# Splitting the 128-row products of one 256-token MLP block into two 64-row tiles of the array

## The chip, the cores and the metric

The kernel runs on one core of one Trainium2 chip. Its time is the device time of one execution in microseconds (us); the comparison is between medians of repeated executions. Five things of the core matter here: TensorE (PE in the rows; PEld is its weight load), VectorE (DVE), ScalarE (ACT), the DMA queues that SyncE (SP) issues to, and the eight banks of PSUM into which TensorE writes.

## The reference, cut to what matters

An attention with a position bias gives x of 2304 tokens by 512; a gated MLP follows:

```python
def _moe_ref(x, w_in, w_out):        # x 2304 x 512, w_in 512 x 2048, w_out 2048 x 512
    h = x @ w_in
    sp = np.where(h > 20.0, h, np.log1p(np.exp(np.minimum(h, 20.0))))
    g = h * np.tanh(sp)
    return (g @ w_out).astype(np.float32)
```

## The kernel before

The first 313 us make the bias, the attention and, beside them, the split weights. The rest is the MLP, which is where the change lies. Each fp32 operand is held as a high and a low part in the type fp32r, and a product is three products: high by high, high by low, low by high.

The tokens are cut into five blocks of 512, 512, 256, 512 and 512 (`blocks`, numbered 0 to 4). The 2048 hidden columns are cut into 16 slices of 128. A *unit* is one slice of a block of 512 tokens, or two slices of the block of 256, so that it always fills a PSUM bank of 128 x 512. There are 72 units; block 2 (256 tokens) has units 32 to 39. For unit k, written H(k), G(k) and P(k) in this document:

- H(k), `hidden`: TensorE computes h of the unit (L553; in block 2, 24 products of 256 columns, in the others 12 of 512), ScalarE takes exp (L558), VectorE clamps it and forms e*(e+2) (L559, L560).
- G(k), `gate`: ScalarE takes a logarithm and an exponential (L568, L569), VectorE multiplies h by e (L570) and that by r (L571), ScalarE writes the high part ghi (L575), VectorE the low part glo (L576).
- P(k), `project`: 12 products of 512 columns add the unit to y (L591). After a block's last unit y is copied out by both engines (L608 on ScalarE, L610 on VectorE) and stored (L611).

The order is written out by hand, and each engine executes its own instructions in that order. One turn of the loop is: in some turns a piece of the next block's x, then H(k), P(k-3), G(k-1). The pieces for the next block: in the turn whose first slice is 6 (unit 35 in block 2), `load_x` and `load_r` issue the loads of x (L307) and of the softmax reciprocals r (L321) through SP's queue, behind whatever that queue still has to issue. In the turns with slice 8 and up (units 36 to 39 in block 2) `split_x` works ahead of H(k): for two of the four rows of x in a turn, first VectorE multiplies x by r (L534) and ScalarE writes the high parts xhi (L535), in units 36 and 37; then VectorE writes the low parts xlo (L537), in units 38 and 39. H(40), the first unit of block 3, reads xhi and xlo.

PSUM: `h_ps` has four banks for h, and a new h takes the bank that was released earliest; `y_ps` has four banks, y0 to y3, of which block 2 uses two. h of unit k is read for the last time by L570 in G(k).

The 64-row slices TOP and LOW already serve the attention's scores, where the two heads of a pair lie in the upper and lower 64 rows:

```python
    TOP, LOW = slice(0, 64), slice(64, P)
    heads = (TOP, KO), (LOW, KO - 64 if c < 4 else KO)
    for j in range(2):
        for s, (rows, k0) in zip(live[n], heads):
            pe.matmul(s[:, j, :SH], q[rows], raw[rows, k0 + j * SH:k0 + (j + 1) * SH], start=True, stop=True)
```

Of the kernel before, what the change touches and what calls it, by code (L numbers as in the profile page):

```python
# [7 lines left out]
F32 = mybir.dt.float32  # L8
# [3 lines left out]
ALU = mybir.AluOpType  # L12
# [5 lines left out]
DM, DFF = 512, 2048  # L18
NT = B * S
P = 128  # L20
# [10 lines left out]
TB = 512  # L31
NFC = DFF // P
# [12 lines left out]
def kernel(ctx: ExitStack, tc, qk, v, wb, w2, w_in, w_out, psia, psi4, rinv, eye, out):  # L45
    nc = tc.nc
    pe, dve, act, pool, sp = nc.tensor, nc.vector, nc.scalar, nc.gpsimd, nc.sync
# [131 lines left out]
    TOP, LOW = slice(0, 64), slice(64, P)  # L179
# [247 lines left out]
    def reach(t):  # L427

        left, right = 16 * t + 15, S - 16 * t
        n = max(left + 1, right)  # L430
        return left, right, n + n % 2
# [6 lines left out]
    for idx, t in enumerate(ts):  # L438
        spent["a"] += 1.0 + (1.9 if idx in SOFT_AT else 0.0)
        spent["v"] += (1.7 if idx in SOFT_AT else 0.0)  # L440
        n = reach(t)[2]
        price = {"v": 0.10 + 0.00072 * n, "a": 0.30 + 0.0008 * n}
        for cg in (3, 2, 1, 0):
            e = min(price, key=lambda k: spent[k] + price[k])
# [32 lines left out]
    for idx in range(NB + 2):  # L477
        if idx < NB:
            t = ts[idx]
            make_h(idx + 2)  # L480
            n = reach(t)[2]
# [36 lines left out]
    mp = sbuf("mp", 2, side="right")  # L518
    h_ps = psum("h_ps", 4, side="right")
# [21 lines left out]
    h_t, gs, ys = {}, {}, {}  # L541
# [2 lines left out]

    def hidden(blk, fs):
        n = blocks[blk][1]
        h = h_ps.tile([P, TB], F32, name="h")
        for u, f in enumerate(fs):
            g4, r = divmod(f, 4)
            k = 0  # L550
            for w, x in ((w_hi, x_hi[blk]), (w_lo, x_hi[blk]), (w_hi, x_lo[blk])):
                for d in range(HP):
                    pe.matmul(h[:, u * n:(u + 1) * n], w["i", g4, d][:, r * P:(r + 1) * P], x[:, d, :n],  # L553
                              start=(k == 0), stop=(k == 11))
                    k += 1

        e = mp.tile([P, TB], F32, name="e", bufs=3)
        act.activation(e, h, AF.Exp)  # L558
        dve.tensor_scalar(e, e, E20, None, op0=ALU.min)  # L559
        dve.scalar_tensor_tensor(e, e, 2.0, e, op0=ALU.add, op1=ALU.mult)  # L560
        h_t[blk, fs] = (h, e)
# [17 lines left out]
    def project(blk, fs):  # L579
        t0, n = blocks[blk]  # L580
        ghi, glo = gs.pop((blk, fs))
        nt = n // P
        if fs[0] == 0:
            ys[blk] = [y_ps.tile([P, DM], F32, name=f"y{t}") for t in range(nt)]
        for t in range(nt):
            for u, f in enumerate(fs):
                g4, r = divmod(f, 4)
                whi, wlo = w_hi["o", g4, r], w_lo["o", g4, r]
                c0 = u * n + t * P
                for k, (g, w) in enumerate(((ghi, whi), (ghi, wlo), (glo, whi))):  # L590
                    pe.matmul(ys[blk][t], g[:, c0:c0 + P], w,  # L591
                              start=(f == 0 and k == 0), stop=(f == NFC - 1 and k == 2))
        if fs[-1] == NFC - 1:
            for t in range(nt):

                if t % 2 == 0:
                    yo = convp.tile([P, 512, 2], U32, name="w64").bitcast(F32).rearrange("p f t -> p (f t)")
                part = yo[:, t % 2 * DM:(t % 2 + 1) * DM]
                rows = out[t0 + t * P:t0 + (t + 1) * P, :]
                if blk == len(blocks) - 1 and t == nt - 1:  # L600

                    dve.tensor_copy(part[:, :DM // 2], ys[blk][t][:, :DM // 2])
                    act.copy(part[:, DM // 2:], ys[blk][t][:, DM // 2:])
                    sp.dma_start(out=rows[:, :DM // 2], in_=part[:, :DM // 2])
                    act.dma_start(out=rows[:, DM // 2:], in_=part[:, DM // 2:])
                    continue
                if t % 2:
                    act.copy(part, ys[blk][t])  # L608
                else:
                    dve.tensor_copy(part, ys[blk][t])  # L610
                sp.dma_start(out=rows, in_=part)  # L611
            del ys[blk]


    step(NS)
    split_x(0, XPARTS)
    hidden(*units[0])
    step(NS + 1)
    step(NS + 2)
# [4 lines left out]
    y_ps = psum("y_ps", 1)  # L624
    alloc_weights(order[EARLY:MIDDLE], wq)
    gate(*units[0], 3)
    hidden(*units[1])
    gate(*units[1], 3)
    hidden(*units[2])

    for k in range(2, len(units) + LAG2):
        if k < len(units):
            blk, fs = units[k]
            f = fs[0]
            if blk + 1 < len(blocks):
                if f == 6:
                    load_x(blk + 1, xp)
                    x_lo[blk + 1] = xp.tile([P, HP, TB], F32R, name="xlo")
                    load_r(blk + 1, x_lo[blk + 1].bitcast(F32), 0, HP)

                if f >= 8:
                    split_x(blk + 1, XPARTS[f - 8:f - 8 + len(fs)])
            if k > 2:
                hidden(blk, fs)
        if k >= LAG2:
            project(*units[k - LAG2])
        if 2 <= k - 1 < len(units):
            gate(*units[k - 1], 2)
# [55 lines left out]
```

## Time and profile before

| | |
|---|---|
| time, median of 3 runs | 725.22 us (723.25 to 726.1) |
| profiled execution, its own time | 724.99 us |
| its span, first to last instruction | 723.2 us |
| PE busy, share of the span | 693.0 us, 96% |
| DVE busy | 509.4 us, 70% |
| ACT busy | 484.3 us, 67% |
| granted TensorE clock, mean | 0.991 of 2.4 GHz |
| block 2 on TensorE, start of H(32) to start of H(40) | 490.50 to 535.47 us |

Busy time is the union of an engine's instructions. A matmul's recorded length contains the way through the array, so matmuls that follow each other overlap in the records; the pace of a stream is read from starts, not from lengths. In a timeline row the first two numbers are the start and the length of a merged group; what stands in brackets is how long the engine was idle before it and what ended that. SPq is SP's queue.

### The profile page before, as it was taken

How to read it: one execution, taken by the hardware profiler on the slowest of the kernel's cores; microseconds unless marked ns; L12 is line 12 of the kernel's file. 1: busy time of each engine (PE TensorE's matmuls, PEld its weight loads, DVE VectorE, ACT ScalarE, POOL GpSimd, SP SyncE). 2: the span in 40 equal slices, each digit the busy share in tenths (PEclk: the TensorE clock that was granted, in tenths of full speed). 3: DMA queues.
4: the chain of work that ended last, by engine and by line, in shares of the span. 5: the costliest groups of instructions: out<-in, count | busy, mean ns of one | idle time of the engine just before them, and what ended most of it. 6: DMA issues, size and time to landing. Idle time of an engine off the chain costs nothing.

```text
span 723.2 us, 12806 instructions
## 1 busy us (share of the span) xinstructions
PE 693.0 (96%) x4768; PEld 508.0 (70%) x4768; DVE 509.4 (70%) x1080; ACT 484.3 (67%) x1059; POOL 11.5 (2%) x14
## 2 busy tenths in 40 slices
PE   6777999999999999989999999999999999999997
PEld 2214666666666666647888888889988888888886
DVE  7983888878888887548879666665577567665554
ACT  6895999898999999876666445544445454454443
POOL 0000110000000000300000000000000000000000
PEclk9998999999999999999999999999999999999999
DMA  4995458556735855204000030000603200010001
GB/s 152 325 309 173 143 195 271 181 162 204 243 134 196 260 203 206 68 17 127 1 0 1 0 118 1 0 1 1 176 0 106 41 0 1 1 58 1 0 2 58
DMA packets 43918, 74.79 MB, mean 103 GB/s; under 512 B 13904, under 2 KB 22608, under 8 KB 43856
## 3 DMA queue, kind: packets, MB, share of 16 engines
q1 hardware_dynamic: 43280, 73.75, 31.6%
q8 instruction: 37, 0.61, 0.3%
q10 hardware_dynamic: 576, 0.22, 0.1%
q14 instruction: 25, 0.20, 0.1%
HBM read 53.55 MB, written 20.40 MB: 102 GB/s over the span
## 4 chain that ended last, share of the span: by engine, by line
PE 69%; ACT 17%; DVE 6%; issue 3%; DMA 3%; SPq 1%; DVEq 0%; ACTq 0%
PE h L553 25%; PE y L591 25%; ACT pt L223 7%; PE o L282 6%; PE s L192 5%; ACT main L263 5%; PE bps L485 3%; PE tp L256 3%; DVE pt L208 2%; DMA bias_d<-bt 2%; PE tp L259 1%; PE o L286 1%; ACT main L268 1%; ACT tail L265 1%; ACT bt L467 1%
## 5 line engine op out<-in xcount | busy, mean ns | idle before, releaser
L208 DVE CUSTOM_DVE_ANT_0 pt<-s,bias 128x576 f32<-128x576 f32 (+1 forms) x160 | 115.9, 754 | 52.0 <-PE s L192 49.2
L223 ACT ACTIVATE pt<-pt,m 128x576 f32<-128x576 f32 x144 | 111.2, 772 | 26.6 <-DVE m L208 21.7
L591 PE MATMUL y<-who,ghi 128*128 128x512 f32 x288 | 112.2, 389 | 0.0
L591 PE MATMUL y<-wlo,ghi 128*128 128x512 f32 x288 | 112.1, 389 | 0.0
L591 PE MATMUL y<-who,glo 128*128 128x512 f32 x288 | 112.0, 389 | 0.0
L192 PE MATMUL s<-rawqk 64*128 64x288 f32 x640 | 108.2, 430 | 2.0 <-DVE m L208 1.9
L575 ACT CAST ghi<-e 128x512 fp32r<-128x512 f32 x72 | 44.7, 621 | 91.7 <-DVE e L571 91.6
L192 PEld LDWEIGHTS s<-rawqk 64*128 64x128 f32 x640 | 63.4, 186 | 44.2 <-DVE m L208 17.3
L558 ACT ACTIVATE e<-h 128x512 f32<-128x512 f32 x72 | 42.8, 596 | 63.0 <-PE h L553 62.8
L553 PE MATMUL h<-xhi,whi 128*128 128x512 f32 (+1 forms) x320 | 79.9, 370 | 1.7 <-ACT xhi L535 1.6
L553 PE MATMUL h<-xlo,whi 128*128 128x512 f32 (+1 forms) x320 | 79.9, 371 | 0.9 <-DVE xlo L537 0.8
L576 DVE TENSOR_TENSOR glo<-e,ghi 128x512 fp32r<-128x512 f32 x72 | 49.8, 691 | 43.5 <-ACT ghi L575 43.5
L559 DVE TENSOR_SCALAR e<-e 128x512 f32<-128x512 f32 x72 | 30.6, 426 | 69.7 <-ACT e L558 69.7
L553 PE MATMUL h<-xhi,wli 128*128 128x512 f32 (+1 forms) x320 | 79.5, 371 | 0.0
L282 PE MATMUL o<-main,vt 128*64 128x320 f32 (+1 forms) x512 | 77.5, 426 | 1.4 <-ACT tail L265 0.7
L256 PEld LDWEIGHTS tp<-ident,pt 64*128 64x128 f32 x1184 | 56.1, 139 | 20.5 <-ACT main L263 10.3
L263 ACT COPY main<-tp 128x512 f32<-128x512 f32 x128 | 67.6, 578 | 0.8 <-PE tp L256 0.3
L553 PEld LDWEIGHTS h<-xhi,whi 128*128 128x128 f32 x320 | 57.3, 188 | 14.0 <-ACT xhi L535 3.1
L256 PE MATMUL tp<-ident,pt 64*128 64x64 f32 x1184 | 62.5, 227 | 4.7 <-ACT main L263 2.2
L553 PEld LDWEIGHTS h<-xlo,whi 128*128 128x128 f32 x320 | 57.4, 190 | 11.8 <-DVE xlo L537 1.6
L553 PEld LDWEIGHTS h<-xhi,wli 128*128 128x128 f32 x320 | 57.4, 190 | 10.1
L591 PEld LDWEIGHTS y<-who,glo 128*128 128x128 f32 x288 | 54.1, 188 | 11.4
(54 smaller groups left out, 883.5 us busy)
## 6 DMA issues: line engine op xcount, KB each, us to landing
rawqk<-in_qk_dram SPq DMA_DIRECT2D x16, 672.0 KB
bias_d<-bt SPq DMA_DIRECT2D x36, 295.5 KB
w<-in_w_in_dram SPq DMA_DIRECT2D x16, 512.0 KB
w<-in_w_out_dram SPq DMA_DIRECT2D x16, 512.0 KB
vt<-in_v_dram SPq DMA_DIRECT2D x16, 320.0 KB
bias<-bias_d SPq DMA_DIRECT2D x16, 288.0 KB
out_dram<-w SPq DMA_DIRECT2D x17, 256.0 KB
bias<-bias_d SPq DMA_DIRECT2D x16, 256.0 KB
```

The costliest lines, as they stand in the source:

```text
L192: pe.matmul(s[:, j, :SH], q[rows], raw[rows, k0 + j * SH:k0 + (j + 1) * SH], start=True, stop=True)
L208: dve.tensor_tensor_reduce(out=halves(pt[rows, sl]), in0=s[rows, :, :SH], in1=halves(bt[rows, sl]), scale=-0.125, scalar=BIG, op0=ALU.add, ...
L223: act.activation(ps, ps, AF.Exp, bias=m[:, u:u + 1], scale=-1.0, accum_out=sums[i][:, k:k + 1])
L256: pe.transpose(tp[:, k * 64:k * 64 + 64], pt[rows, c0:c0 + P], ident[rows, rows])
L263: act.copy(main[:, :, :, q0:q0 + 64], tp.rearrange("p (h k q) -> p h k q", h=2, k=4))
L282: pe.matmul(o[h * 64:h * 64 + 64, :w], vt[:, h, k, :], main[:, h, k, :], start=(k == 0), stop=False, **kw)
L553: pe.matmul(h[:, u * n:(u + 1) * n], w["i", g4, d][:, r * P:(r + 1) * P], x[:, d, :n], start=(k == 0), stop=(k == 11))
L558: act.activation(e, h, AF.Exp)
L559: dve.tensor_scalar(e, e, E20, None, op0=ALU.min)
L575: act.copy(ghi, e)
L576: dve.tensor_tensor(glo, e, ghi.bitcast(F32), op=ALU.subtract)
L591: pe.matmul(ys[blk][t], g[:, c0:c0 + P], w, start=(f == 0 and k == 0), stop=(f == NFC - 1 and k == 2))
```

## The change

In block 2 (n = 256) each product over 128 rows becomes two over 64 rows, upper and lower, issued one behind the other, with a bank each. The two halves of h are added (ScalarE copies the lower half to e, VectorE adds it to the upper half in PSUM) ahead of the exponential. The halves of y go to y0/y2 and y1/y3 and are added when block 2 is copied out. The other blocks keep their products.

```diff
     def hidden(blk, fs):
         n = blocks[blk][1]
-        h = h_ps.tile([P, TB], F32, name="h")
+        rows = (TOP, LOW) if n < TB else (slice(0, P),)
+        hs = [h_ps.tile([P, TB], F32, name="h") for _ in rows]
...
                 for d in range(HP):
-                    pe.matmul(h[:, u * n:(u + 1) * n], w["i", g4, d][:, r * P:(r + 1) * P], x[:, d, :n],
-                              start=(k == 0), stop=(k == 11))
+                    for h, p in zip(hs, rows):
+                        pe.matmul(h[:, u * n:(u + 1) * n], w["i", g4, d][p, r * P:(r + 1) * P], x[p, d, :n],
+                                  start=(k == 0), stop=(k == 11))
                     k += 1
-
+        h = hs[0]
         e = mp.tile([P, TB], F32, name="e", bufs=3)
+        if n < TB:
+            act.copy(e, hs[1])
+            dve.tensor_tensor(h, h, e, op=ALU.add)
+
         act.activation(e, h, AF.Exp)
...
         if fs[0] == 0:
-            ys[blk] = [y_ps.tile([P, DM], F32, name=f"y{t}") for t in range(nt)]
+            ys[blk] = [y_ps.tile([P, DM], F32, name=f"y{t}") for t in range(4)]
+        rows = (TOP, LOW) if n < TB else (slice(0, P),)
...
                 for k, (g, w) in enumerate(((ghi, whi), (ghi, wlo), (glo, whi))):
-                    pe.matmul(ys[blk][t], g[:, c0:c0 + P], w,
-                              start=(f == 0 and k == 0), stop=(f == NFC - 1 and k == 2))
+                    for j, p in enumerate(rows):
+                        pe.matmul(ys[blk][t + 2 * j], g[p, c0:c0 + P], w[p],
+                                  start=(f == 0 and k == 0), stop=(f == NFC - 1 and k == 2))
...
-                if t % 2:
+                if n < TB:
+                    act.copy(part, ys[blk][t])
+                    dve.tensor_tensor(part, part, ys[blk][t + 2], op=ALU.add)
+                elif t % 2:
                     act.copy(part, ys[blk][t])
```

The added lines move the numbers of those behind them; in the rows below L555, L561 and L562 are the changed kernel's product, copy and add of `hidden`, L564 its exponential, L576 its product h*e, L621 its copy of y by VectorE.

On TensorE at the start of H(37), before: the last two products of P(33) (y1), then the first of H(37), whose h is h_6331.

```order
L591 MATMUL y1_6250<-wlo03_4737,ghi_6202 128x512
L591 MATMUL y1_6250<-who03_4736,glo_6203 128x512
L553 MATMUL h_6331<-xhi_5733,whi20_4740 128x256 [waits PE_49]
L553 MATMUL h_6331<-xhi_5733,whi21_4742 128x256
L553 MATMUL h_6331<-xhi_5733,whi22_4744 128x256
```

The same place of the changed kernel; h_6492 and h_6493 are the upper and the lower half.

```order
L599 MATMUL y1_6358<-who03_4736,glo_6284 128x512
L599 MATMUL y3_6360<-who03_4736,glo_6284 128x512
L555 MATMUL h_6492<-xhi_5733,whi20_4740 128x256 [waits DVE_49]
L555 MATMUL h_6493<-xhi_5733,whi20_4740 128x256 [waits Activation_49]
L555 MATMUL h_6492<-xhi_5733,whi21_4742 128x256
```

Each product stands twice, and the two first ones have a wait for the bank: the upper half takes the bank whose last reader is L576 of G(34), the lower half the one whose last reader is ScalarE's copy L561 of H(36). The same holds for the other units of block 2, each time with L576 of three units before and L561 of the unit before.

On ScalarE around unit 36, before: G(34)'s high part, the two xhi of `split_x`, the exponential of H(36) (h_6277), and G(35).

```order
L575 CAST ghi_6264<-e_6175 128x512 [waits DVE_49,PE_49]
L535 CAST xhi_6272<-xraw_6210 128x512 [waits DMAHW6_49,DMAHW5_49,DVE_49]
L535 CAST xhi_6272<-xraw_6210 128x512 [waits DVE_49]
L558 ACTIVATE e_6302<-h_6277 128x512 [waits PE_49]
L568 ACTIVATE r_6318<-e_6245,two_73 128x512
```

The same place of the changed kernel, where h_6399 and h_6400 are the halves of H(36):

```order
L581 CAST ghi_6386<-e_6254 128x512 [waits DVE_49,PE_49]
L535 CAST xhi_6394<-xraw_6291 128x512 [waits DMAHW6_49,DMAHW5_49,DVE_49]
L535 CAST xhi_6394<-xraw_6291 128x512 [waits DVE_49]
L561 COPY e_6449<-h_6400 128x512 [waits PE_49]
L564 ACTIVATE e_6449<-h_6399 128x512 [waits DVE_49]
L574 ACTIVATE r_6479<-e_6351,two_73 128x512
```

The copy that releases the lower bank stands behind both xhi, and the exponential now waits for VectorE instead of TensorE.

On VectorE around the copying out of block 1, before: clamp and product of H(34), then y0 and y2.

```order
L559 TENSOR_SCALAR e_6175<-e_6175 128x512 [waits Activation_49]
L560 SCALAR_TENSOR_TENSOR e_6175<-e_6175 128x512 [waits DVE_49]
L610 COPY w64_6191<-y0_5546 128x512 [waits PE_49]
L610 COPY w64_6196<-y2_5548 128x512 [waits PE_49]
```

The same place of the changed kernel:

```order
L562 TENSOR_TENSOR h_6204<-h_6204,e_6254 128x512 [waits Activation_49]
L565 TENSOR_SCALAR e_6254<-e_6254 128x512 [waits Activation_49]
L566 SCALAR_TENSOR_TENSOR e_6254<-e_6254 128x512 [waits DVE_49]
L621 COPY w64_6272<-y0_5546 128x512 [waits PE_49]
L621 COPY w64_6277<-y2_5548 128x512 [waits PE_49]
```

The add of the halves has come in ahead of the clamp, and the copies of y stand behind all three.

## Rows read from the trace of the kernel before

**Rows 1.** The page, its chain that ended last, shares of the span by line.

```profile
PE h L553 25%; PE y L591 25%; ACT pt L223 7%; PE o L282 6%; PE s L192 5%; ACT main L263 5%; PE bps L485 3%; PE tp L256 3%; DVE pt L208 2%; DMA bias_d<-bt 2%; PE tp L259 1%; PE o L286 1%; ACT main L268 1%; ACT tail L265 1%; ACT bt L467 1%
```

**Rows 2.** Block 2: length, busy time of PE, PEld, DVE, ACT, POOL, clock, DMA.

```profile
490.50:535.47 44.97, 44.97 (x290) 41.02 (x288) 26.16 (x43) 20.47 (x34) 0.00 (x0) 1.00 0.25 71
```

**Rows 3.** TensorE's timeline: H(37), P(34) and the start of H(38).

```profile
518.60 0.64 PE L553 MATMUL h<-xhi,whi 128*128 128x256 f32 x4
...
521.47 0.40 PE L591 MATMUL y<-who,ghi 128*128 128x512 f32 x1
...
524.22 0.64 PE L553 MATMUL h<-xhi,whi 128*128 128x256 f32 x4
```

**Rows 4.** TensorE's timeline: H(40) and the start of P(37).

```profile
535.47 1.07 PE L553 MATMUL h<-xhi,whi 128*128 128x512 f32 x4
...
538.70 1.10 PE L553 MATMUL h<-xlo,whi 128*128 128x512 f32 x2 [0.81 <-DVE xlo L537]
539.64 0.40 PE L591 MATMUL y<-who,ghi 128*128 128x512 f32 x1
```

**Rows 5.** The chain that ended last in order of time, 500 to 545 us.

```profile
507.56 0.59 ACT w L608
...
513.82 5.91 DMA xlo<-r_d
...
538.04 1.22 DVE xlo L537 x2
539.30 0.50 PE h L553
```

**Rows 6.** ScalarE's, VectorE's and SP's timelines, from the end of H(34) on.

```profile
504.81 0.60 ACT L558 ACTIVATE e<-h 128x512 f32<-128x512 f32 x1 [1.73 <-PE h L553]
...
505.44 0.43 DVE L559 TENSOR_SCALAR e<-e 128x512 f32<-128x512 f32 x1 [1.63 <-ACT e L558]
505.90 0.69 DVE L560 SCALAR_TENSOR_TENSOR e<-e 128x512 f32<-128x512 f32 x1
506.51 1.28 DVE L610 COPY w<-y 128x512 f32<-128x512 f32 x2
...
507.22 1.81 SPq L611 DMA_DIRECT2D out_dram<-w  x4
509.08 1.26 SPq L307 DMA_DIRECT2D xraw<-x_d  x2
```

**Rows 7.** All instructions by line and shape: busy us, mean ns, idle before.

```profile
L570 DVE TENSOR_TENSOR e<-h,e 128x512 f32<-128x512 f32 x72 | 49.2, 684 | 5.3 <-ACT r L568 5.3
...
L608 ACT COPY w<-y 128x512 f32<-128x512 f32 x8 | 4.7, 587 | 9.5 <-PE y L591 9.5
```

**Rows 8.** VectorE's and ScalarE's timelines at units 36 to 38.

```profile
520.12 1.29 DVE L534 TENSOR_TENSOR xraw<-xraw,xlo 128x512 f32<-128x512 f32 x2 [4.57 <-DMA xlo<-r_d]
...
521.97 0.59 ACT L558 ACTIVATE e<-h 128x512 f32<-128x512 f32 x1
...
528.34 0.59 ACT L558 ACTIVATE e<-h 128x512 f32<-128x512 f32 x1
...
532.13 0.59 ACT L558 ACTIVATE e<-h 128x512 f32<-128x512 f32 x1
```

**Rows 9.** TensorE in the attention: timelines of two windows that start alike.

```profile
305.42 0.71 PE L282 MATMUL o<-main,vt 128*64 128x320 f32 x4
306.06 0.51 PE L192 MATMUL s<-rawqk 64*128 64x288 f32 x2
...
306.06 1.24 PE L192 MATMUL s<-rawqk 64*128 64x288 f32 x8
```

**Rows 10.** Weight loads of the 64-row transposes, their timeline.

```profile
303.31 0.57 PEld L256 LDWEIGHTS tp<-ident,pt 64*128 64x128 f32 x15 [0.35 <-ACT main L263]
```

**Rows 11.** TensorE's timeline at H(0), and the clock in it (columns as in 2).

```profile
316.55 2.26 PE L553 MATMUL h<-xhi,whi 128*128 128x512 f32 x4 [1.61 <-ACT xhi L535]
...
318.30:321.60 3.30, 3.30 (x9) 2.52 (x9) 0.73 (x2) 0.00 (x0) 0.00 (x0) 0.50 0.00 0
```

## The prediction

> **What bounds the kernel now.** The chain that ended last, by line, comes first: the MLP's two products carry half of the span [rows 1], so what changes in block 2 counts if TensorE feels it. Then block 2 by itself: from the start of H(32) to the start of H(40) TensorE is busy 44.97 of 44.97 us at the granted clock 1.00, the level of 2.4 GHz; VectorE has 26.16 and ScalarE 20.47 us of work in it [rows 2]. TensorE's timeline gives the pace: H(37) takes 521.47 - 518.60 = 2.87 us for 24 products, 0.12 us each; P(34) takes 524.22 - 521.47 = 2.75 us for 12, 0.23 us each [rows 3]. At 2.4 GHz 256 columns are 0.107 us and 512 are 0.213 us, so a product costs its columns and about 0.013 us.
>
> But the chain in order of time shows that it leaves TensorE in just this block: from the copy of block 1's y (507.56) through the stores and loads of SP's queue, the landing of the reciprocals r (a piece of 5.91 us), VectorE's first L534, the units 36 to 39 on ScalarE and VectorE, to L537 and the end of H(40) at 539.30 [rows 5]. VectorE stood idle 4.57 us for r; ScalarE, which has xhi ahead of the exponential in its order, does exp of H(36) only at 521.97, when TensorE has long begun H(37), and exp of H(37) at 528.34 [rows 8]. TensorE runs ahead of this on its free h banks and pays once: H(40) to P(37) is 4.17 us in place of 12 x 0.227 = 2.72, so 1.45 us, with L537 as the releaser [rows 4]. ScalarE and VectorE are thus a second path through block 2, with under 2 us of slack against TensorE's.
>
> **The change part by part.**
>
> *The pairs.* 192 products of H and 96 of P become pairs. The nearest rows are the attention's scores, 64-row tiles in fp32: two passes together take 0.51 us and eight take 1.24 us, so pairs end (1.24 - 0.51) / 3 = 0.243 us apart [rows 9]. That pace alone would also fit one pass behind the other at a column per cycle (288 / 2.4 = 0.12 us each), but then two would not lie within the 0.51 us of the first: the halves run side by side, at two cycles per column. I take side by side for fp32r too, at its one cycle per column, so that a pair costs what the full product cost. In these rows the fixed part is smaller: 0.243 us is 2 x 288 cycles and 0.003 us. If that small part comes with the half tile and not with the type, a pair saves 0.0108 us, at most 288 x 0.0108 = 3.1 us. I take no saving, since the 0.013 us belong to the type that stays, and keep the other end for the range.
>
> *The changes of tile.* From the last 128 x 64 pass of L282 (the second of its pairs starts at 305.42 + 0.71 - 0.43 = 305.70; the pace there is 0.27) to the 64-row L192 at 306.06 are 0.36 us, 0.09 us over the pace [rows 9]. Block 2 has 14 such changes, since H(32) to H(34) alternate with P of block 1 and P(37) to P(39) with H of block 3: 1.3 us, of which five lie ahead of the copying out of block 1, two more fall into the wait below, and seven (0.65 us) come behind it.
>
> *Copy and add of h, and the loads.* The copy is like L608 (0.587 us), the add like L570 (0.684 us) [rows 7]; with two hand-overs of some 0.05 us, 1.4 us ahead of each exponential of block 2. In unit 34 they stand ahead of clamp and product, and behind these VectorE copies block 1's y0 and y2 without a gap (L559 at 505.44, L560, L610 at 506.51); SP's four stores wait for that, and the loads stand behind the stores, the first at 509.08 [rows 6]. So loads and landing come 1.4 us later, and 5 x 0.09 = 0.45 us with TensorE: L534 starts at X = 520.12 + 1.85 = 521.97.
>
> *The wait at H(37).* Its lower half needs the bank that ScalarE's copy of H(36) frees, and that copy stands behind xhi, so behind L534, so behind r. It comes where exp of H(36) stood, 521.97 - 520.12 = 1.85 us behind L534 [rows 8] (by chance the size of the shift too). With its 0.59 us and a hand-over TensorE goes on at X + 2.53. H(37) began 1.52 us ahead of L534 before (518.60): 4.05 us lost. Queued behind it on TensorE is all the rest.
>
> *The wait at H(38).* H(37) and P(34) after that restart end at X + 2.53 + 5.62 = X + 8.15. ScalarE's copy of H(37) stands where exp stood, 528.34 - 521.97 = 6.37 us after the one of unit 36 [rows 8], plus the 1.4 us that copy and add put into that round: X + 1.85 + 7.77 = X + 9.62, released at X + 10.3. So 2.15 us are lost. H(39): the copy of H(38) comes 3.79 us after exp of H(37) before (532.13) [rows 8], plus 1.4, so X + 14.8 and released at X + 15.5; TensorE arrives at X + 15.9, nothing lost. H(33) to H(36) find their banks: the copy ends 0.7 us after the H before them, and P lies between with 2.7 us.
>
> *H(40).* L537 moves by the same 1.85 us and three rounds of 1.4 us, to 538.04 + 1.22 + 6.05 = 545.3 [rows 5], X + 23.35; TensorE begins H(40) at X + 15.9 + 5.62 + 0.09 = X + 21.6 and needs L537's last piece eleven products later, at 546.1. The 1.45 us of [rows 4] vanish.
>
> *Copying out block 2.* Two copies and two adds where there was one copy each: under 2 us, covered by the 2.7 us of H(43), and block 3's P needs y2 and y3 later still.
>
> *The clock.* H(37) waits some 5 us. After an idle time of 1.61 us and four slow products the clock stood at 0.50, the level of 1.2 GHz, for the 3.30 us shown, within H(0) [rows 11]. A fall of that length costs half, about 1.7 us; ahead of H(38) it would vanish in the 2.15 us there. I take 0 and keep 1.7 us for the range.
>
> Sum: 1.4 + 0.45 + 4.05 + 2.15 - 1.45 + 0.65 = 7.25 us. On the profiled execution's 724.99 us (its span is 1.8 us less; the median of the three runs is 0.2 us more) that is **732.3 us**, 1.0% slower.
>
> If a pair does save 0.0108 us, that comes through only where TensorE isn't waiting behind it: the 72 pairs of H(32) to H(34) ahead of the loads, then H(38), P(35), H(39), P(36) and P(37) to P(39), 180 of the 288 pairs, 1.95 us: 730.3 us.
>
> **The rivals.**
>
> *The halves don't run side by side in fp32r.* Speaks for it: no row has fp32r in a half tile. Against it: the common start in [rows 9]. Then H takes 2.87 us more, P 2.72, eight times each, 44.7 us; r is covered, the 1.45 us vanish, the changes of tile cost 1.1: 724.99 + 44.7 - 1.45 + 1.1 = 769 us. A milder form is that only the weight loads of a pair wait for each other. From the full product's pace a load of 128 columns fits into 0.12 us, so a pair of H would be at most 0.24 us, and P's 0.24 for 0.227: 23 + 1.3 - 1.45 + 1.1 gives 749 us. Against it: fifteen such loads of 64 rows took 0.57 us, under 0.04 each [rows 10].
>
> The Trainium skill bears on this rival (TensorE: Matmul & The Clock Gate, LDWEIGHTS (loading the stationary operand)): a load costs its columns at 1.2 GHz however few rows it has, 107 ns for 128, so half tiles double the loading. By that figure, loads in a row, a pair of H would be 0.213 us, H 17.9 us longer in all, and the sum about 743 us as an estimate; the trace's 0.04 us contradicts the queue, not the size of one load.
>
> *Not slower.* The second path doesn't reach TensorE and the saving of 0.0108 us per pair is real: 724.99 - 3.1 + 1.3 - 1.45 = 721.7 us. It decides by one thing, when L534 starts: without waits H(40) would begin at 535.47 + 0.65 - 2.7 (eight H and five P with the saving) = 533.4 and need L537's last piece at 535.9, which ends at X + 23.35, so r would have to land by 512.5 in place of 520.1. The last load was issued only at 513.82 [rows 5]; I see nothing that brings it forward.
>
> **How the numbers follow.** Forecast (pairs side by side, r exposed): 80%, with its own range 729 to 736, from the saving and an earlier landing (-3) to a fall of the clock and one more wait like H(38)'s (+3.7). Halves or loads in a row: 13%, 743 to 769. Not slower: 7%. A change under 0.5% (3.6 us) can't be told from none in this kernel. The range 726.5 to 738 goes past the first case's own to both sides and leaves out the other two. Faster by over 0.5% (below 721.6) is half of the last case, 3%; within 0.5% the other half and the lowest edge of the first, 9%; slower 88%.
>
> **What would show it.** After: H(32) 2.87 us for 24 pairs (2.6 with the saving, 5.7 in a row); SP's first load some 1.8 us later, at 511; a wait of TensorE from about 519 to 524.5, released by ScalarE's copy, and one of 2 us at H(38); H(40) without its wait; 0.09 us at each change of tile. Wrong would make it: r landing much earlier or later than 12.6 us after the last copy of block 1's y began (507.56 to 520.12), a pair's pace off 0.12 us, a clock that stays low past H(38).

## The result, and the profile after

The changed kernel takes **733.95 us** (median of 4 runs, 733.1 to 736.27), the kernel before 724.75 us beside it: a ratio of **1.0133, interval 1.0101 to 1.0164**. That is 9.2 us more; forecast were 7.25 us more, 732.3 us, and a range of 726.5 to 738. The profiled execution took 733.88 us, span 732.1 us.

The traces differ ahead of block 2: H(32) starts at 490.50 before [rows 2] and at 489.26 with the change, and between 488.1 and 492.0 us in the twelve traces of this study (one for each kernel), though the code up to there is the same. So traces are compared below from the start of H(32): how much later H(43) starts, the first unit behind the last change of tile. Before that is 62.77 us, with the change 72.76: **9.99 us more**.

The page's chain that ended last, by line, answers to [rows 1]:

```profile
PE h L555 26%; PE y L599 25%; PE s L192 6%; PE o L282 6%; ACT pt L223 6%; ACT main L263 4%; PE tp L256 3%; PE bps L485 3%; DMA bias_d<-bt 2%; DVE pt L208 2%; PE tp L259 1%; PE o L286 1%; ACT main L268 1%; DMA xlo<-r_d 1%; ACT tail L265 1%
```

The reciprocals' transfer is in the list for the first time. In the windows, the first one from H(32) to H(40) as in [rows 2], the second the stretch of the low clock:

```profile
489.26:544.22 54.96, 48.16 (x541) 43.53 (x540) 32.24 (x52) 25.44 (x43) 0.00 (x0) 0.94 0.21 59
...
521.10:527.90 6.80, 2.83 (x26) 2.84 (x28) 3.45 (x6) 3.54 (x6) 0.00 (x0) 0.50 0.01 4
```

H(32) to H(40) has grown from 44.97 to 54.96 us. TensorE, busy throughout before, has 6.80 us of idle time in it; VectorE has 6.1 and ScalarE 5.0 us more work; the granted clock stood at 0.50, the level of 1.2 GHz, for 6.80 us. All idle time of TensorE between 490 and 560 us is in one group of its waits (in total, times, longest):

```profile
PE h L555 <- ACT e L561: 6.8, 2, 6.2
```

L561 is the copy of the lower half of h. TensorE's timeline, with the pace of the pairs, the changes of tile and both waits (the counts are of half tiles):

```profile
495.26 0.74 PE L555 MATMUL h<-xhi,whi 64*128 64x256 f32 x8
...
498.32 0.50 PE L599 MATMUL y<-who,ghi 128*128 128x512 f32 x1
...
512.98 0.64 PE L555 MATMUL h<-xhi,whi 64*128 64x256 f32 x8
...
515.85 0.40 PE L599 MATMUL y<-who,ghi 64*128 64x512 f32 x2
...
518.60 0.27 PE L555 MATMUL h<-xhi,whi 64*128 64x256 f32 x1
525.07 1.22 PE L555 MATMUL h<-xhi,whi 64*128 64x256 f32 x7 [6.20 <-ACT e L561]
...
529.28 0.39 PE L599 MATMUL y<-who,ghi 64*128 64x512 f32 x1
...
531.90 0.27 PE L555 MATMUL h<-xhi,whi 64*128 64x256 f32 x1
532.79 0.74 PE L555 MATMUL h<-xhi,whi 64*128 64x256 f32 x7 [0.60 <-ACT e L561]
...
544.22 1.20 PE L555 MATMUL h<-xhi,whi 128*128 128x512 f32 x4
...
547.19 0.50 PE L599 MATMUL y<-who,ghi 64*128 64x512 f32 x2
...
550.16 1.20 PE L555 MATMUL h<-xhi,whi 128*128 128x512 f32 x4
```

H(36), among half tiles on both sides, takes 515.85 - 512.98 = 2.87 us and P(32) 518.60 - 515.85 = 2.75 us, to the hundredth what full products take [rows 3]. H(33), with a change of tile at its start and end, takes 498.32 - 495.26 = 3.06 us, 0.19 more; H(40) and P(37) take 2.97 each where a turn of block 3 needs 2.72. At H(37) the first product of the upper half starts and the lower half waits; 525.07 - 518.60 - 0.12 = 6.35 us of the stream are lost; H(38) then takes 0.88 us more than its 2.87. H(40) runs through, where [rows 4] had a wait.

The chain in order of time (start, length, what) answers to [rows 5]:

```profile
504.43 0.60 ACT e L561
...
505.05 0.71 DVE h L562
505.78 0.61 ACT e L564
...
507.57 1.20 DVE w L621 x2
...
515.59 6.26 DMA xlo<-r_d
...
522.58 0.70 DVE xraw L534
523.31 1.22 ACT xhi L535 x2
524.53 0.49 ACT e L561
...
532.25 0.49 ACT e L561
...
532.79 3.14 PE h L555 x47
```

It goes through copy and add of H(34), the copies of y, SP's queue, the landing of r, L534, xhi and the copies of H(36) and H(37) to TensorE. SP's timeline answers to the last two of [rows 6]:

```profile
508.20 2.54 SPq L622 DMA_DIRECT2D out_dram<-w  x4
510.79 1.27 SPq L307 DMA_DIRECT2D xraw<-x_d  x2
512.16 4.53 SPq L321 DMA_DIRECT2D xlo<-r_d  x6
```

The same four stores took 1.81 us to issue before and take 2.54 now.

### The profile page after: what moved, and what is told of

It is laid out like the page before. It is cut to its first block, busy times and chain, and to the rows that moved or that the text cites. A ratio compares the mean times of both kernels' runs of the same rounds, so it can differ in the third digit from the quotient of the medians.

```text
span 732.1 us, 13399 instructions
## 1 busy us (share of the span) xinstructions
PE 696.7 (95%) x5056; PEld 509.4 (70%) x5056; DVE 515.5 (70%) x1089; ACT 489.7 (67%) x1068; POOL 12.0 (2%) x14
## 4 chain that ended last, share of the span: by engine, by line
PE 72%; ACT 15%; DVE 5%; issue 3%; DMA 3%; SPq 1%; DVEq 0%; ACTq 0%
PE h L555 26%; PE y L599 25%; PE s L192 6%; PE o L282 6%; ACT pt L223 6%; ACT main L263 4%; PE tp L256 3%; PE bps L485 3%; DMA bias_d<-bt 2%; DVE pt L208 2%; PE tp L259 1%; PE o L286 1%; ACT main L268 1%; DMA xlo<-r_d 1%; ACT tail L265 1%
## 5 line engine op out<-in xcount | busy, mean ns | idle before, releaser
L599 PE MATMUL y<-who,ghi 128*128 128x512 f32 (+1 forms) x320 | 114.2, 392 | 0.0
L599 PE MATMUL y<-wlo,ghi 128*128 128x512 f32 (+1 forms) x320 | 113.5, 389 | 0.0
L599 PE MATMUL y<-who,glo 128*128 128x512 f32 (+1 forms) x320 | 113.5, 389 | 0.0
L555 PE MATMUL h<-xhi,whi 128*128 128x512 f32 (+1 forms) x384 | 82.8, 364 | 8.4 <-ACT e L561 6.8
L564 ACT ACTIVATE e<-h 128x512 f32<-128x512 f32 x72 | 42.8, 596 | 67.5 <-PE h L555 58.4
L555 PE MATMUL h<-xhi,wli 128*128 128x512 f32 (+1 forms) x384 | 80.8, 358 | 0.0
L555 PE MATMUL h<-xlo,whi 128*128 128x512 f32 (+1 forms) x384 | 80.0, 356 | 0.0
L555 PEld LDWEIGHTS h<-xhi,whi 128*128 128x128 f32 (+1 forms) x384 | 58.2, 192 | 23.3 <-ACT e L561 7.4
L555 PEld LDWEIGHTS h<-xhi,wli 128*128 128x128 f32 (+1 forms) x384 | 58.6, 192 | 10.2
L555 PEld LDWEIGHTS h<-xlo,whi 128*128 128x128 f32 (+1 forms) x384 | 58.3, 191 | 10.2
L599 PEld LDWEIGHTS y<-who,ghi 128*128 128x128 f32 (+1 forms) x320 | 55.4, 187 | 12.0 <-issue 0.7
```

What stands on the lines that cost most here:

```text
L555: pe.matmul(h[:, u * n:(u + 1) * n], w["i", g4, d][p, r * P:(r + 1) * P], x[p, d, :n], start=(k == 0), stop=(k == 11))
L599: pe.matmul(ys[blk][t + 2 * j], g[p, c0:c0 + P], w[p], start=(f == 0 and k == 0), stop=(f == NFC - 1 and k == 2))
```

## The experiments

Theory A is the prediction's: copy and add lengthen the path over ScalarE and VectorE, which is late from r's landing on, TensorE meets it, and the halves themselves cost only the changes of tile. Rivals put the loss in the half tiles, in the two banks that a unit needs, or in r's landing alone. "Later" is how much later H(43) starts, counted from H(32) as above; this column and the last come from one trace of each kernel, the medians from several executions. In the edits, three dots stand for lines left out.

| kernel | median us | ratio, 95% | H(43) later, us | first L534 after H(32), us |
|---|---|---|---|---|
| before | 724.71 to 725.3 | 1 | 0 | 29.62 |
| changed | 733.95 | 1.0133 [1.0101, 1.0164] | 9.99 | 33.32 |
| x1 copy and add, no split | 731.7 | 1.0089 [1.0059, 1.0120] | 7.62 | 31.57 |
| x2 split, no copy and add | 728.65 | 1.0039 [1.0019, 1.0059] | 3.56 | 31.88 |
| x3 P alone | 726.47 | 1.0012 [0.9993, 1.0030] | 1.80 | 29.99 |
| x4 before, loads early | 723.77 | 0.9973 [0.9955, 0.9991] | -1.49 | 24.98 |
| y1 changed, loads early | 731.12 | 1.0082 [1.0055, 1.0108] | 5.73 | 27.57 |
| y2 split_x behind H | 733.52 | 1.0125 [1.0084, 1.0166] | 9.45 | 33.44 |
| y3 H alone | 733.81 | 1.0122 [1.0082, 1.0162] | 9.03 | 33.36 |
| y4 H alone, spare banks | 733.17 | 1.0115 [1.0076, 1.0153] | 8.27 | 33.83 |
| z1 halves four by four | 734.71 | 1.0128 [1.0101, 1.0155] | 11.06 | 33.94 |
| z2 H split from unit 35 | 733.91 | 1.0115 [1.0087, 1.0142] | 8.07 | 31.09 |

### x1: copy and add without a split

The kernel before, with h copied to e and added to itself in block 2; h is doubled there, so this part of the output is another.

```diff
         e = mp.tile([P, TB], F32, name="e", bufs=3)
+        if n < TB:
+            act.copy(e, h)
+            dve.tensor_tensor(h, h, e, op=ALU.add)
```

> The kernel before with full 128-row products, and in block 2 only ScalarE's copy of h and VectorE's add ahead of the exponential (h is added to itself, so the output isn't the reference's; the work and its order are those of the changed kernel). Theory A (the second path: copy and add on ScalarE and VectorE, behind the wait for r, make H(40) late): r lands 1.4 us later, three more rounds of 1.4 us, so L537 ends 5.6 us later and H(40)'s wait grows from 1.45 to about 7 us: 730.3 us, +0.8%. Theory B (the loss sits on TensorE: the half tiles and their banks): within 0.5 us of the kernel before, 725 us.

Measured: 731.7 us, 6.8 us over the kernel before beside it (724.9), with no half tile and no second bank for h. TensorE's waits from 489 to 566 us:

```profile
PE h L553 <- DVE xlo L537: 2.2, 1, 2.2
PE y L595 <- ACT ghi L579: 2.2, 2, 2.0
```

With four banks for full products TensorE runs further ahead, so it meets the late path at P(35), P(36) and H(40) in place of H(37). Behind the two long waits the granted clock stood at 0.50 for 3.4 us each time. The windows are P(35) and P(37), with the columns of [rows 2]:

```profile
527.61:532.06 4.45, 4.45 (x12) 3.34 (x13) 2.62 (x5) 2.38 (x5) 0.00 (x0) 0.62 0.00 0
544.05:548.39 4.34, 4.34 (x14) 3.40 (x12) 2.79 (x6) 2.65 (x5) 0.00 (x0) 0.61 0.00 0
```

Where they took 2.75 and 2.74 us before, they now take 4.45 and 4.34, so some 3.3 of the 7.62 us are the price of the clock. Theory B's 725 us fell. Copy and add on their own, with the falls of the clock that their waits bring, make three quarters of the loss.

### x2: the split without copy and add

The lower half of h is computed and left out of the sum.

```diff
-        if n < TB:
-            act.copy(e, hs[1])
-            dve.tensor_tensor(h, h, e, op=ALU.add)
```

> The changed kernel without copy and add of h (the lower half of h is left out of the result; its products are still made). Theory A: the second path moves only by the changes of tile ahead of the loads; TensorE pays 14 changes of tile of 0.2 us, 2.8 us, of which up to 1.45 us takes the place of H(40)'s wait: 726 to 728 us, no wait at H(37) and H(38). Theory B: still near 734 us.

Measured: 728.65 us. No wait at H(37); 3.56 us of delay, of which the changes of tile make about 3, and waits of 1.5 us for L572 (h*e, the last reader of the upper half's bank) take what H(40)'s vanished wait gives. These waits stand at H(38) (1.05 us) and H(39) (0.49 us), and theory A had none at H(38). Otherwise it is theory A's course, a little over its figure.

### x3: only P split

H stays a full product, without copy and add; y is split and summed as changed.

```diff
-        hs = [h_ps.tile([P, TB], F32, name="h") for _ in rows]
+        h = h_ps.tile([P, TB], F32, name="h")
...
```

> Only P of block 2 is split, H keeps its full products: every P of block 2 then stands between full products, 16 changes of tile at 0.19 to 0.25 us, 3.0 to 4.0 us, and ScalarE's and VectorE's path is that of the kernel before. Theory A: H(40)'s wait of 1.45 us is eaten by the lateness of TensorE, so 726.3 to 727.5 us. At the predicted 0.09 us a change it would be 725 us. If half tiles cost something beyond the change of tile, more than 728 us.

Measured: 726.47 us, and TensorE has no wait at all between 489 and 560 us. This is the cleanest price of a change of tile. Turns H(38), P(35) and H(41) in the chain in order of time:

```profile
518.09 3.06 PE h L553 x24
521.14 2.94 PE y L593 x24
...
542.02 2.97 PE h L553 x12
```

With 16 changes H(43) is 1.80 us later though the 1.45 us at H(40) [rows 4] are gone: (1.80 + 1.45) / 16 = 0.20 us a change, 0.19 in block 2's turns, 0.25 beside block 3's products.

### x4: the kernel before with its loads early

```diff
-                if f == 6:
+                if f == (2 if blocks[blk][1] < TB else 6):
```

The loads of x and r for block 3 are issued in unit 33's turn, ahead of the stores of block 1 in SP's queue.

> The kernel before, with the loads of x and r for block 3 issued in unit 33 in place of unit 35, which puts them ahead of the four stores of block 1's y in SP's queue. Theory A: r lands before VectorE wants it, VectorE's 4.57 us of idleness and H(40)'s wait of 1.45 us go: 723.3 us, -0.2%. If the wait was not r's, no change (724.8).

Measured: 723.77 us, 0.9973 [0.9955, 0.9991], the only version that beats both kernels. L534 starts 4.6 us earlier, and the chain of H(39), P(36), H(40) has no wait left:

```profile
528.15 2.87 PE h L553 x24
531.03 2.75 PE y L591 x12
533.77 2.72 PE h L553 x12
```

So r's landing was the late end of the second path in the kernel before.

### y1: the changed kernel with its loads early

The edit of x4 on the changed kernel.

> The changed kernel with the loads for block 3 issued in unit 33 in place of unit 35, ahead of the stores of block 1's y. Theory A (r's landing plus the longer rounds on ScalarE and VectorE): the wait of some 6 us at H(37) goes; left are 14 changes of tile of 0.2 us less the 1.45 us of H(40), +1.4 us, and up to 2 us because a round with xhi, copy and add takes ScalarE and VectorE 7.7 us (525 to 532 us in the changed kernel's trace) against TensorE's 5.6: 726 to 729 us. Theory B (the loss is local to TensorE, half tiles and banks): 733 us.

Measured: 731.12 us, a miss: 2.8 us are won, not 5 or more. L534 starts 5.75 us earlier than in the changed kernel, and TensorE waits for the copy all the same. Its waits and H(38) in its timeline:

```profile
PE h L555 <- ACT e L561: 2.3, 2, 1.8
```

```profile
526.56 0.27 PE L555 MATMUL h<-xhi,whi 64*128 64x256 f32 x1
528.68 0.74 PE L555 MATMUL h<-xhi,whi 64*128 64x256 f32 x7 [1.84 <-ACT e L561]
```

From the copy of H(36) to that of H(37) ScalarE and VectorE need 7.7 us (h's copy and add, xhi, L534 and the gate, one behind the other), TensorE 5.62 for its turn. So a second cause stands behind r: in the turns with xhi the round itself is too long. The granted clock then stood at 0.50 for 3.4 us (530.0 to 533.4), which made H(38) and P(35) some 1.6 us longer. Theory B's 733 us is missed by about as much, to the other side.

### y2: split_x behind H

In block 2, L534, L535 and L537 stand behind the copy, add and exponential of the same turn.

```diff
-                if f >= 8:
+                if f >= 8 and blk != 2:
...
             if k > 2:
                 hidden(blk, fs)
+            if f >= 8 and blk == 2:
+                split_x(blk + 1, XPARTS[f - 8:f - 8 + len(fs)])
```

> The changed kernel with the pieces of block 3's x (L534, xhi, xlo) written behind H in the turns of units 36 to 39, so that ScalarE's copy of H(36) and VectorE's add no longer stand behind r. The loads stay where they are. Theory A: r lands as late as in the changed kernel, but copy, add, exponential, clamp and product of unit 36, some 3 us, are done ahead of it: H(37) doesn't wait, H(38) and H(40) still do, 729 to 731.5 us. Theory C (the order in ScalarE's queue that holds the lower bank is the whole loss): all 6.8 us of bank waits go, 727 us.

Measured: 733.52 us; both theories missed the time. The wait at H(37) is gone, as theory A had it, and comes back at H(38), H(39) and H(40):

```profile
PE h L555 <- ACT e L561: 2.1, 2, 1.6
PE h L555 <- DVE e L576: 1.7, 1, 1.7
PE h L555 <- DVE xlo L537: 1.3, 1, 1.3
```

The order in front of the bank decides where TensorE meets the path, not how long the path is: L537 is done no earlier, 56.9 us after the start of H(32) as against 56.5 in the changed kernel. Theory A's figure had left that out.

### y3 and y4: only H split, then with spare banks

y3 keeps P as before; y4 also puts the lower halves of units 35 to 39 into the banks y2 and y3, which block 2 then doesn't use.

```diff
-            ys[blk] = [y_ps.tile([P, DM], F32, name=f"y{t}") for t in range(4)]
+            ys[blk] = [y_ps.tile([P, DM], F32, name=f"y{t}") for t in range(nt)]
...
```

```diff
-        hs = [h_ps.tile([P, TB], F32, name="h") for _ in rows]
+        hs = [h_ps.tile([P, TB], F32, name="h")]
+        if n < TB:
+            late = fs[0] >= 6
+            hs.append(y_ps.tile([P, TB], F32, name=f"y{2 + fs[0] // 2 % 2}") if late else h_ps.tile([P, TB], F32, name="h"))
```

> Only H of block 2 is split, P keeps its full products and y its two banks. 16 changes of tile in place of 14, the second path as in the changed kernel, the copying out as before: all theories 733 to 735 us. It is the base for the next run.

> As the run with only H split, with the lower halves of units 35 to 39 in the two banks of y that block 2 leaves free, so that a lower half has its bank two units after the copy and not one. Theory A (the second path sets the end, the bank only the place where TensorE meets it): H(37) and H(38) wait little, H(40) waits for L537 instead, some 5 us; at most 1 us is gained on the run with only H split. Theory C (the shortage of banks is the cause): 6 to 7 us are gained, 727 us.

Measured: 733.81 and 733.17 us. y3 has the wait at H(37) (5.5 us). In y4 it is gone, and these stand in its place:

```profile
PE y L600 <- ACT ghi L584: 2.5, 2, 1.4
PE h L558 <- DVE xlo L537: 2.2, 1, 2.2
PE y L558 <- ACT w L617: 0.4, 1, 0.4
```

(The last one is H(35), whose lower half waits until block 1's y3 is copied out by L617.) Two more banks are worth at most 0.8 us, which theory A had and theory C's 727 us had not, though H(40) waits 2.2 us and not 5. As in y2, the wait moves and the loss stays.

### z1: the halves four by four

```diff
-                for d in range(HP):
-                    for h, p in zip(hs, rows):
+                for h, p in zip(hs, rows):
+                    for d in range(HP):
...
```

> The changed kernel, with another order of the products of H in block 2: of each term the four products of the upper half, then the four of the lower half, in place of one of each in turn. Same products, same banks. Theory A: the halves of block 2 cost nothing extra in the changed kernel because a lower half runs beside the upper one issued just ahead of it (pairs 0.12 us apart), and a second product on the same 64 rows waits for the first. Then of eight half products only the two in the middle lie side by side: seven times 0.12 us in place of four, H about 5.0 us in place of 2.87 (5.7 if none lies beside another), some 17 to 23 us over eight units, less what the waits at H(37) and H(38) shrink (about 5 us): 743 to 751 us, H(38) without a wait. Rival B: half products are at full pace by themselves, since 64 rows need half the time or the array takes the two queues in any order: H 2.9 us and 733 to 735 us as the changed kernel.

Measured: 734.71 us, H(36) again 2.87 us: theory A's idea that a half runs beside the one issued just ahead of it fell, rival B held. TensorE's timeline at H(37) shows how:

```profile
521.61 0.63 PE L555 MATMUL h<-xhi,whi 64*128 64x256 f32 x4
528.39 0.58 PE L555 MATMUL h<-xhi,whi 64*128 64x256 f32 x1 [6.15 <-ACT e L561]
528.40 0.58 PE L555 MATMUL h<-xhi,wli 64*128 64x256 f32 x1
528.77 0.41 PE L555 MATMUL h<-xhi,whi 64*128 64x256 f32 x1
528.78 0.41 PE L555 MATMUL h<-xhi,wli 64*128 64x256 f32 x1
```

In the program the order is four upper whi, four lower whi, four upper wli. The four upper ones ran at 521.61; then a lower whi and an upper wli start 0.01 us apart, and so on in pairs, each with its own weights: the upper half is ahead of the lower by four products, and starts out of the program's order. Of rival B's two reasons these rows show the second.

### z2: H split from unit 35 on

```diff
+        split = n < TB and fs[0] >= 6
-        rows = (TOP, LOW) if n < TB else (slice(0, P),)
+        rows = (TOP, LOW) if split else (slice(0, P),)
...
-        if n < TB:
+        if split:
```

> The changed kernel with H split from unit 35 on alone; H(32) to H(34) are full products without copy and add, all else as changed. Measured from the start of H(32), the first L534 stood at 29.62 us before and at 33.32 us with the change, where 1.85 us more had been forecast. Theory A: all of the 3.7 us comes from what stands ahead of the loads (tile changes of H(32) to H(34), copy and add of H(34), and the stores and loads of SP that they push): L534 at 29.6 to 30.5 us here, the wait at H(37) stays (about 4 us), and the kernel takes 729.5 to 731 us, 3 to 4.5 us less than the changed one. Rival B: part of the late landing comes from elsewhere, such as the copies beside it or block 2's P: L534 at 32 us or later, 732 us or more.

Measured: 733.91 us, not to be told from the changed kernel, where theory A had 729.5 to 731; in the trace it is 1.9 us shorter from H(32) on. SP's timeline:

```profile
507.97 1.81 SPq L623 DMA_DIRECT2D out_dram<-w  x4
509.82 1.26 SPq L307 DMA_DIRECT2D xraw<-x_d  x2
511.18 4.66 SPq L321 DMA_DIRECT2D xlo<-r_d  x6
```

Stores and loads stand where they stood before (the loads 18.58 us after H(32), in both), and L534 still comes 1.47 us later than before. At 31.09 us it lies between what the two theories expected: 2.2 of the 3.7 us come from the work ahead of the loads, the rest from the loads' own issue and landing, and the wait at H(37) is still 5.0 us.

## Why the prediction came out

It was right in its size and in its mechanism, with two terms of the sum too small. From the start of H(32) to that of H(43) it had 7.25 us, measured are 9.99. About 1.85 of the difference come from X, the start of L534, which moved twice as far as forecast, and 1.0 from the seven changes of tile behind the waits (some 1.7 us in place of 0.65).

- **Two paths, the second with little slack.** Right: the chain of the changed kernel runs over SP's queue, r, L534, xhi and the copy. x1 shows it without half tiles, x4 from the other side.
- **Pairs side by side, no saving.** Right: 2.87 and 2.75 us, in every kernel with half tiles. The saving of 0.0108 us per pair isn't there, nor the rival of halves or loads in a row. The two loads of a pair lie side by side too: those of H(36)'s first pair take 0.19 us together, as long as one load of a full product before (mean 0.188 us).

```profile
512.98 0.19 PEld L555 LDWEIGHTS h<-xhi,whi 64*128 64x128 f32 x2
```

The Trainium skill (TensorE: Matmul & The Clock Gate, LDWEIGHTS (loading the stationary operand)) has 107 ns for one load of 128 columns, as an estimate by its formula; two of them in a row would not fit into a pair's 0.12 us, which agrees with loads side by side. But the prediction was wrong that [rows 10] leave that figure standing: fifteen loads in 0.57 us are one per 0.08 us in each half even two at a time, faster than the figure allows, and the measurement decides.
- **Changes of tile.** The price was read wrong. 0.09 us is the delay of the first 64 x 128 product behind the 128 x 64 ones of the attention [rows 9]; a second part lies behind that first product. In the same place of the kernel before, the second pair starts at 306.40, 0.34 us behind the first, where the pairs' pace is 0.243:

```profile
306.40 0.89 PE L192 MATMUL s<-rawqk 64*128 64x288 f32 x6
```

That is 0.10 us more, so a change costs 0.19 us in the attention too, though its types and shapes are others. Block 2 shows the same second part: the first eight half products of H(33), behind a change, take 0.74 us, those of H(36) 0.64. For 14 changes the sum had 1.3 us; between the two starts they cost 2.9. At 0.19 us each, five in X and seven behind the waits, the sum would have been some 8.4 us.
- **Copy and add ahead of the loads (X).** VectorE's copies of y start 2.22 us later after H(32) than before: 1.4 as forecast and 0.8 of tile changes in place of 0.45. Not foreseen were 0.73 us that SP's four stores took longer, and some 0.7 us in the loads' issues and their landing; they are nearly all that the sum lacks once the changes of tile are priced right. X moved by 3.70, not 1.85. The 12.6 us from the last copy of y to L534, whose change the prediction had named as a sign of being wrong, became 14.5 (508.09 to 522.58).
- **H(37).** Released by ScalarE's copy, at X + 2.49 (forecast X + 2.53; with a hand-over of 0.05 us its terms give 2.49). The lost time is 6.35 us where the terms gave 5.3 (from 519.2, with the tile changes, to 524.5), because X came 1.85 us later than forecast and TensorE reached H(37) only 0.6 later.
- **H(38).** Released at X + 10.21 (forecast X + 10.3). TensorE came at X + 9.32 in place of X + 8.15, so 0.9 us were lost in place of 2.15: it lost the rest to the clock.
- **The clock.** It fell within the wait, at 521.10, and stood at 0.50 until 527.90, 2.83 us into the work behind it, so H(37)'s remaining pairs took 529.16 - 525.07 = 4.09 us, 1.34 more than at full pace. That vanished in the wait at H(38), as the prediction had it, because the copy of H(37) stands behind xhi and started only at 532.16, some 2.7 us after H(37) was done: both waits and the clock together are 8.57 us, against 7.4.
- **H(39), H(40), copying out.** No wait, as forecast; the 1.45 us of [rows 4] are gone. L537 ended at X + 23.2 (forecast X + 23.35) and H(40) began at X + 21.64 (forecast X + 21.6).
- **Not slower.** The saving that this rival needs isn't there. It also asked for r by 512.5, which is L534 some 22.0 us after H(32); no run brought it so early in a split kernel. y1 came to 27.57, 2 us earlier than the kernel before, and is still 0.8% slower. y1 also shows what the rival had left out: the round of 7.7 us on ScalarE and VectorE, which an early r doesn't shorten.

Why the single issues of SP took longer stays open.

## What to carry to other kernels

Here the half tiles of a full product were no faster than the product; what they add behind it (copy, add, a bank) counts on the path of the evacuating engines, and that path has to be laid beside TensorE's turn by turn before an edit on TensorE is priced. A wait on a PSUM bank that is removed, by order or by spare banks, comes back elsewhere as long as the late path keeps its length; shorten the path, as the earlier loads did. Read the price of a change of tile from one turn to the next and not up to the first start behind it, since half of it lay behind the first product here, and count how often the loop alternates.

## What the runs showed of the hardware

- A change between 128 x 128 and 64 x 128 tiles costs 0.19 us between turns of 256 and 512 columns and 0.25 us beside 512-column products of block 3, on average 0.20 (x3), with no wait in the records. About half of it stands ahead of the first product of the new tile, the rest between that product and the next; in the attention the two parts are 0.09 and 0.10 us.
- The two row halves are worked off as two streams: in z1 one is four products ahead of the other, and their starts leave the program's order. In y4, where the lower half's bank is named y, the 13th product of H(35)'s upper half starts at 509.04, ahead of the 12th of its lower half at 509.05. The Trainium skill (TensorE: Matmul & The Clock Gate, Part 3: Packing small matmuls — row/col tiling) says that matmuls start and end in the program's order; the starts in these rows differ, and the measurement decides.
- SP's four stores of block 1 took 1.81 us to issue in the kernel before and in x1, x2, x3 and z2 (2.06 in x4), but 2.54 to 3.04 us in all six kernels where H(34) is split and summed; one store took 1.07 to 1.65 us in place of about 0.4. What holds it isn't in the records.
- The length of a fall of the granted clock did not follow the length of the wait. With waits of 6.20 us (changed kernel), 6.15 (z1), 5.5 (y3) and 5.0 (z2) it stood at 0.50 for 6.8, 10.2, 3.4 and 6.8 us, and behind y1's wait of 1.84 us for 3.4.
